# Second layer of an attention and expert kernel: an earlier token load, other places for the sinkhorn steps and weight splits, and three blocks rescaled on POOL

## The chip, the cores and the metric

The kernel runs on one core of a Trainium2 chip. The core has TensorE (PE: matrix products; its weight loads are shown apart as PEld), VectorE (DVE), ScalarE (ACT), GpSimd (POOL) and SyncE (SP), which here only issues DMAs. The metric is the device time of one execution in microseconds. The kernel before was run three times; of one more execution there is a profile.

## The reference

Three layers follow each other on 3072 tokens of width 512: chunked attention, an expert layer in which each token goes to at most one of 8 experts, and a second expert layer in which every token goes through all 8 experts, weighted by a matrix P that sinkhorn steps have balanced. The change lies in the last one:

```python
logits = x @ w_gate
P = np.exp(logits - logits.max())
for _ in range(8):
    P /= P.sum(1, keepdims=True) + 1e-09
    P /= P.sum(0, keepdims=True) + 1e-09
    P *= N / E
out = np.zeros((N, D))
for e in range(E):                       # 8 experts, D = 512, F = 1024
    ye = np.maximum(x @ w1[e], 0.0) @ w2[e]
    out += P[:, e:e + 1] * ye
```

All of it is in fp32. The kernel gets fp32 precision out of TensorE by splitting each operand into a high and a low part and adding three products.

## The kernel before

The order of the instructions of every engine is written out by hand; each engine runs its own in that order and waits on semaphores. A tile whose buffer is used again waits for the last user of that buffer.

**Blocks and units.** The second layer goes expert by expert (e) over six blocks of 512 tokens (s). Expert and block together are a block number b = 6e + s, and each has two halves of F, so unit n = 2b + half runs from 0 to 95; 12 units are an expert (`EU`). A product of 512x512 by 512x512 is made with seven products of quarter size instead of eight (Strassen's way): `h_mm(n, i)` is one of the seven products x @ w1 of unit n, `y_mm(n, i)` one of the seven h @ w2. Each is 12 matmuls of 128x256. In step n of the main loop (lines 1253 to 1315) TensorE makes the h products of unit n and, between them, the y products of unit n - 1, in the order `TURN` (line 40): h0, y, h1, y, h5, h4, y, h6, y, h3, h2, y, y, end. The y products come in the order `YORD`; the one behind h6 accumulates in the PSUM bank `y3`. In a step with even n two more y products follow (`y_tail`).

**What the other engines do in a step.** `h_done` (line 961) takes the h products out of PSUM: after h0 ACT copies the bank to a second one (line 964, called the seed copy here, since the further products are added onto it), after h6 VectorE adds r22 (line 954) and ACT and VectorE split it into high and low part (`c_hi`, `c_lo`: cb3), and after h2 VectorE makes the sum u (line 987) and four combinations that are split in turn. The bank of h0 is needed again by the next step's h0, so that waits for u; the bank of h3 waits for r22. In even steps `y_done` copies the first y product into the tile oB (ACT), and `y_end`, behind h0 of the next step, scales the parts of a block by P, adds them into oA and oB and stores them (`keep_out`): from block 6 on with an accumulating DMA issued by POOL (line 1058), before that with a DMA of SP.

**Blocks 0 and 1** of expert 0 are finished before P is known. They are kept unscaled in DRAM (`yd`), loaded later into oA and oB (`fix_load`), multiplied by P on VectorE and stored (`fix_store`), in steps 11 and 13.

**P.** `sink_max1` and `sink_exp` in step 1 take the maximum and the exponential, `sink_a` divides by the row sums. Each `sink_c` has a product with ones on TensorE into bank `y3` (line 901), then four VectorE operations; `sink_a` has four more. The eight steps lie in steps 3 and 5, behind h0, h1, h5 and h4 (lines 1230 to 1232).

**Later tokens.** During expert 0, odd steps prepare the next block: 16 transposes (`prep_trans`), four sums on POOL (`prep_sums`, into oA and oB), and seven splits (`prep_split`: ACT copies, VectorE subtracts), numbers 4 and 6 behind h2 and number 2 at the end. From block 5 on, `x_read` loads the seven split operands of the next block from DRAM in odd steps.

**Weights.** The eight pieces of the next expert are converted while the last unit of an expert and the first two of the next run: four subtractions on POOL for a piece (line 218), then four splits, each an ACT cast (line 204) and a VectorE subtraction (line 208). `QUOTA` (line 1251) says how many splits stand behind which h product, for n mod 12 = 11, 0 and 1.

**The start.** Lines 1149 to 1153 load the four w2 pieces of expert 0 into tiles that are needed later for other things; then line 1160 loads the first block's tokens (`x2n`, out of `x_t`, which the layer before fills by scatter DMAs of POOL), and line 1161 the logits (out of `l_t`, filled by further scatters). In unit 0 the h products go in the order `START` (0, 3, 1, 5, 6, 4, 2); lines 1203 to 1214 put sums and eight weight splits between them.

Of the kernel before, what the change touches and what calls it, by code (L numbers as in the profile page):

```python
# [8 lines left out]
F32 = mybir.dt.float32  # L9
# [4 lines left out]
ALU = mybir.AluOpType  # L14
# [20 lines left out]
EU = NS * 2  # L35
# [11 lines left out]
def kernel(ctx, tc, qT, kT, v, mem_kT, mem_v, wg, m1_w1, m1_w2, m2_w1, m2_w2, out):  # L47
    nc = tc.nc
# [291 lines left out]
    i = 0  # L340
# [505 lines left out]
    ones_f = m2.tile([128, 128], F32, name="ones_f")  # L846
    nc.gpsimd.memset(ones_f, 1.0)
    xd = [dram.tile([7, 128, 1024], F32, name=f"xd{s}") for s in range(NS)]
    yd = [dram.tile([2, 128, 1024], F32, name=f"yd{s}") for s in range(2)]
    add = lambda o, a, b: nc.vector.tensor_tensor(out=o, in0=a, in1=b, op=ALU.add)  # L850
    xn = {}
    xs = {}
# [1 line left out]
    def x2_load(sb):  # L854
        for h in range(2):
            xn[sb, h] = raw.tile([128, 2, D], F32, name="x2n", tag="wraw", bufs=3)
            r = 512 * sb + 256 * h
            nc.sync.dma_start(out=xn[sb, h], in_=x_t[r:r + 256, :].rearrange("(j p) d -> p j d", p=128))
# [41 lines left out]
    def sink_c(p):  # L900
        nc.tensor.matmul(p[:, 0:NT * E], ones_f, P.rearrange("p t e -> p (t e)"), start=True, stop=True)
        nc.vector.tensor_reduce(out=c_s, in_=p[:, 0:NT * E].rearrange("p (t e) -> p e t", e=E), axis=AX.X, op=ALU.add)
        nc.vector.tensor_scalar(out=c_s, in0=c_s, scalar1=1e-9, scalar2=float(E) / N, op0=ALU.add, op1=ALU.mult)
        nc.vector.reciprocal(out=c_s, in_=c_s)
        nc.vector.tensor_tensor(out=P, in0=P, in1=c_s.unsqueeze(1).to_broadcast(LS), op=ALU.mult)
# [28 lines left out]
    def h_mm(n, i, late=False):  # L934
        e, s, half = where_is(n)
        x = xs[s, i].rearrange("p h (k t) -> p h k t", k=2)
        new = i in (0, 4)
        if new:
            hb["a"] = bank("h_ps", "h0")
        p = hb["a" if i in (0, 1, 4, 2) else "b"]  # L940
        if late and i == 3:
            p, new = hb["d"], True
        if late and i == 0:
            nc.tensor.matmul(hb["b"], wt[E + e, 0, 0][0][:, 0, 0], xs[s, 0][:, 0], start=True, stop=True, skip_group_check=True)
        for f in range(2):
            wh, wl = wt[E + e, 0, 2 * half + f]
            o = p[:, 256 * f:256 * f + 256]
            for k in range(2):
                nc.tensor.matmul(o, wh[:, i, k], x[:, 0, k], start=(new and f == 0 and k == 0), stop=False, skip_group_check=True)  # L949
                nc.tensor.matmul(o, wh[:, i, k], x[:, 1, k], start=False, stop=False, skip_group_check=True)  # L950
                nc.tensor.matmul(o, wl[:, i, k], x[:, 0, k], start=False, stop=(k == 1), skip_group_check=True)  # L951
# [75 lines left out]
    def scaled(b, h, d, src):  # L1027
        e, s = divmod(b, NS)
        o = O[b, h][:, :, d]
        if b < 2:  # L1030
            if src is not None:
                nc.scalar.copy(out=o, in_=src)
            return
        for j in range(2):
            nc.scalar.activation(out=o[:, j], in_=(o if src is None else src)[:, j], func=ACTF.Copy, scale=P[:, 4 * s + 2 * h + j, e:e + 1])

    def plus(b, h, d, src):
        e, s = divmod(b, NS)
        o = O[b, h][:, :, d]
        if b < 2:  # L1040
            add(o, src, o)
            return
        for j in range(2):
            stt(o[:, j], src[:, j], P[:, 4 * s + 2 * h + j, e:e + 1], o[:, j], ALU.mult, ALU.add)
# [5 lines left out]
    def keep_out(b, h):  # L1050
        e, s = divmod(b, NS)
        o = O[b, h].rearrange("p j d f -> p j (d f)")
        if b < 2:
            nc.sync.dma_start(out=yd[s][h].rearrange("p (j d) -> p j d", j=2), in_=o)
        elif b < NS:
            nc.sync.dma_start(out=rows_of(s, h), in_=o)
        else:
            nc.gpsimd.dma_start(out=rows_of(s, h), in_=o, accum_op=ALU.add)  # L1058
# [35 lines left out]
    def fix_store(s):  # L1094
        for h in range(2):
            t = fixes[s, h].rearrange("p j d f -> p j (d f)")
            for j in range(2):
                nc.vector.tensor_scalar(out=t[:, j], in0=t[:, j], scalar1=P[:, 4 * s + 2 * h + j, 0:1], scalar2=None, op0=ALU.mult)
            nc.sync.dma_start(out=rows_of(s, h), in_=t)


# [45 lines left out]


    HOME = {0: ("cb5", 1, ("cb4",)), 1: ("cb2", 1, ("cb6",)), 2: ("cb1", 3, ("oA",)), 3: ("cb1", 3, ("wraw",))}
    for g in range(NG):  # L1150
        tag, bufs, _ = HOME[g]
        fetched[E, 1, g] = m2.tile([128, 1024], F32, name=tag, tag=tag, bufs=bufs)
        nc.sync.dma_start(out=fetched[E, 1, g], in_=m2_w2[0, g])
# [3 lines left out]
        d = [(raw if t == "wraw" else m2).tile([128, 1024], F32, name=t, tag=t, bufs=3 if t == "wraw" else 1) for t in tags]  # L1157
        conv_subs(E, 1, g, fetched[E, 1, g], (d[0][:, 0:512], d[0][:, 512:1024]))

    x2_load(0)  # L1160
    nc.sync.dma_start(out=P, in_=l_t.rearrange("(t p) e -> p t e", p=128))
    ps0 = {}
    for h, k in ((0, 0), (1, 0), (1, 1), (0, 1)):
# [29 lines left out]
    def start4():  # L1193
        x_hi(0, 2, sums[:, 0])

    def start2():
        x_lo(0, 2, sums[:, 0])

    between = {1: start5, 3: start6, 4: start4, 5: start2}
    hb["b"] = bank("h_ps", "h1")  # L1200
    hb["d"] = bank("h_ps", "y5")
    todo = []
    for k, i in enumerate(START):
        if k in between:
            between[k]()
        h_mm(0, i, True)
        h_done(0, i, True)
        if k in (3, 4):
            first_subs(k - 3)
            todo.append(w2_parts(E, k - 3))  # L1210
        if k in (4, 5):
            for q in todo:
                q.pop(0)()
                q.pop(0)()
# [12 lines left out]

    todo += [first_w2(2), first_w2(3)]
    sinks = {(1, "h0"): lambda p: (nc.vector.tensor_reduce(out=m_p, in_=P, axis=AX.XY, op=ALU.max), sink_max1(p)), (1, "h1"): sink_exp}
    for n in (3, 5):  # L1230
        for c in ("h0", "h1", "h5", "h4"):
            sinks[n, c] = sink_c if (n, c) == (5, "h4") else lambda p: (sink_c(p), sink_a())


    jobs = []
# [12 lines left out]
            todo.clear()  # L1248
            fetch()

    QUOTA = {EU - 1: {"h0": 2, "h1": 2, "h4": 2, "h6": 2}, 0: {"h0": 4, "h1": 4, "h4": 3, "h6": 3}, 1: {"h1": 3, "h4": 4, "h6": 3}}
    later = []
    for n in range(1, NU2 + 1):
        e, s, half = where_is(n)
        b = n // 2
        last = n == NU2
        m = n - 1
        k = n % EU
        nx = b + 1
        ends = half == 0  # L1260
        more = QUOTA.get(n if n < 1 else k, {})
        if n == EU - 2:
            limit[0] = len(order)
            for _ in range(3):
                fetch()
        if k == EU - 1 and e < E - 1:
            jobs += PIECES(e + 1)
            conv_subs(*jobs[0], fetched[jobs[0]])
        if n == 1:
            more = {"h0": 2, "h1": 2, "h5": 2, "h4": 2, "h6": 2}  # L1270
        assert n != 2 or not todo
        yq = list(YORD)
        if half == 0 and nx < NS and n > 1:
            x2_load(nx)
        prep = half == 1 and nx < NS
        for c in TURN:
            if c == "y":
                i = yq.pop(0)
                y_mm(m, i)
                if ends:  # L1280
                    y_done(m // 2, i)
            elif c == "end":
                if not last:
                    h_rest(n)
                    if prep:
                        prep_split(nx, 2)
                if ends and n > 1:
                    y_tail(m // 2)
                    later.append(lambda b=m // 2: y_end(b))
                if last:  # L1290
                    later.pop()()
                if n in (EU - 1, EU + 1):
                    fix_store((n - EU + 1) // 2)
            elif not last:
                i = int(c[1])
                h_mm(n, i)
                h_done(n, i)
                if later:
                    later.pop()()
                if (n, c) in sinks:  # L1300
                    sinks[n, c](bank("g_ps", "y3"))
                if n in (EU - 1, EU + 1) and c == "h4":
                    fix_load((n - EU + 1) // 2)
                if prep:
                    if c in ("h5", "h4"):
                        for h in range(2):
                            prep_trans(nx, h, ("h5", "h4").index(c))
                    if c == "h4":
                        prep_sums(nx)
                    for i in {"h6": (0, 1), "h3": (5, 3), "h2": (4, 6)}.get(c, ()):  # L1310
                        prep_split(nx, i)
                elif half == 1 and nx < E * NS:
                    x_read(nx % NS, i)
                for _ in range(more.get(c, 0)):
                    next_part()
# [43 lines left out]
```

## Time and profile before

| | |
|---|---|
| median of 3 runs | 2452.69 us (2451.85 to 2453.39) |
| the profiled execution | 2452.1 us, its span 2450.4 us |
| busy share of the span: PE, DVE, ACT, POOL | 95%, 62%, 49%, 21% |
| mean granted clock of TensorE | 0.978 of full speed |
| matmuls | 19522 |
| moved by DMA | 343 MB, 140 GB/s on the mean |

The span runs from the first to the last instruction of the profiled execution. The second layer fills it from about 380 us on. A row of the timeline gives the start, the duration, the engine, the line of the kernel, the operation, output<-input, the count of instructions that were merged, and in brackets the idle time of that engine just before and what ended it. A row of lines gives busy time and mean nanoseconds of one, and behind the second bar the idle time before them. A row of windows gives the two ends, the length, the busy time (and count) of PE, PEld, DVE, ACT and POOL, the granted clock, the busy share of the DMA engines and GB/s. Granted clock 1.00 is 2.4 GHz and 0.50 is 1.2 GHz.

### The profile page before, as it was taken

How to read it: one execution, taken by the hardware profiler on the slowest of the kernel's cores; microseconds unless marked ns; L12 is line 12 of the kernel's file. 1: busy time of each engine (PE TensorE's matmuls, PEld its weight loads, DVE VectorE, ACT ScalarE, POOL GpSimd, SP SyncE). 2: the span in 40 equal slices, each digit the busy share in tenths (PEclk: the TensorE clock that was granted, in tenths of full speed). 3: DMA queues.
4: the chain of work that ended last, by engine and by line, in shares of the span. 5: the costliest groups of instructions: out<-in, count | busy, mean ns of one | idle time of the engine just before them, and what ended most of it. 6: DMA issues, size and time to landing. Idle time of an engine off the chain costs nothing. (4 is left out here: it accounts for less than half of the span.)

```text
span 2450.4 us, 48134 instructions
## 1 busy us (share of the span) xinstructions
PE 2316.6 (95%) x19522; PEld 2268.6 (93%) x19522; DVE 1508.6 (62%) x2519; ACT 1200.4 (49%) x2488; POOL 509.4 (21%) x563
## 2 busy tenths in 40 slices
PE   8989994899989998999999999999999999999997
PEld 7879983889989998999899999999999999999997
DVE  5756564776785558555855585558555865576554
ACT  6744543445554445444544454445444554455443
POOL 4432233110230005000500050004101410141000
PEclk9989997999999999999999999999999999999999
DMA  9956643233462526353544355344534462535252
GB/s 236 255 147 200 203 135 133 95 128 140 151 245 79 155 82 177 121 144 90 164 138 123 111 145 157 103 130 133 169 95 138 122 180 82 151 121 155 79 155 35
DMA packets 154349, 343.25 MB, mean 140 GB/s; under 512 B 44489, under 2 KB 56905, under 8 KB 154123
## 3 DMA queue, kind: packets, MB, share of 16 engines
q1 hardware_dynamic: 128202, 289.35, 34.6%
q0 software_dynamic: 25920, 50.77, 12.4%
q8 instruction: 155, 2.54, 0.4%
q14 instruction: 72, 0.58, 0.1%
HBM read 256.71 MB, written 85.10 MB: 139 GB/s over the span
## 5 line engine op out<-in xcount | busy, mean ns | idle before, releaser
L949 PE MATMUL h_ps<-xs,wh 128*128 128x256 f32 x2688 | 766.9, 285 | 65.1 <-DVE r L850 46.3
L950 PE MATMUL h_ps<-xs,wh 128*128 128x256 f32 x2688 | 766.5, 285 | 0.0
L951 PE MATMUL h_ps<-xs,wl 128*128 128x256 f32 x2688 | 763.6, 284 | 0.0
L1018 PE MATMUL y_ps<-wh,cb 128*128 128x256 f32 x2304 | 650.7, 282 | 0.0
L1019 PE MATMUL y_ps<-wl,cb 128*128 128x256 f32 x2304 | 649.5, 282 | 0.0
L1020 PE MATMUL y_ps<-wh,cb 128*128 128x256 f32 x2304 | 648.2, 281 | 0.0
L949 PEld LDWEIGHTS h_ps<-xs,wh 128*128 128x128 f32 x2688 | 514.2, 191 | 72.2 <-DVE r L850 43.0
L951 PEld LDWEIGHTS h_ps<-xs,wl 128*128 128x128 f32 x2688 | 513.6, 191 | 0.0
L950 PEld LDWEIGHTS h_ps<-xs,wh 128*128 128x128 f32 x2688 | 511.5, 190 | 0.0
L915 DVE TENSOR_TENSOR cb<-r,cb 128x512 fp32r<-128x512 f32 x384 | 270.3, 713 | 278.1 <-ACT cb L925 272.0
L1020 PEld LDWEIGHTS y_ps<-wh,cb 128*128 128x128 f32 x2304 | 437.8, 190 | 0.0
L1018 PEld LDWEIGHTS y_ps<-wh,cb 128*128 128x128 f32 x2304 | 437.5, 190 | 0.0
L1019 PEld LDWEIGHTS y_ps<-wl,cb 128*128 128x128 f32 x2304 | 435.8, 189 | 0.0
L1058 POOL DMA_DIRECT2D out_dram<-oA x42 | 50.8, 1209 | 1362.6 <-ACT r L916 960.3
L925 ACT CAST cb<-r 128x512 fp32r<-128x512 f32 x384 | 239.4, 623 | 110.5 <-DVE r L917 86.5
L916 ACT ACTIVATE cb<-r 128x512 fp32r<-128x512 f32 x96 | 60.7, 632 | 288.0 <-DVE r L850 288.0
L916 ACT ACTIVATE r<-h_ps 128x512 f32<-128x512 f32 x191 | 114.3, 598 | 136.0 <-PE h_ps L951 135.3
L850 DVE TENSOR_TENSOR r<-h_ps,m 128x512 f32<-128x512 f32 x97 | 66.8, 689 | 180.5 <-PE h_ps L951 179.2
L208 DVE TENSOR_TENSOR wl<-wraw,wh 128x512 fp32r<-128x512 f32 (+2 forms) x150 | 144.4, 979 | 48.1 <-ACT wh L204 47.2
L218 POOL TENSOR_TENSOR wtt<-wraw 128x256 f32<-128x256 f32 x120 | 136.4, 1137 | 109.4 <-DVE wl L208 92.9
L964 ACT COPY h_ps<-h_ps 128x512 f32<-128x512 f32 x96 | 54.8, 571 | 197.9 <-PE h_ps L951 197.9
L915 DVE TENSOR_TENSOR r<-r,r 128x512 f32<-128x512 f32 x192 | 138.5, 722 | 3.3
(236 smaller groups left out, 3675.5 us busy)
## 6 DMA issues: line engine op xcount, KB each, us to landing
xs<-xd SPq DMA_DIRECT2D x294, 512.0 KB
wraw<-in_m_w_dram SPq DMA_DIRECT2D x124, 512.0 KB
xd<-xs SPq DMA_DIRECT2D x42, 512.0 KB
out_dram<-oA POOLq DMA_DIRECT2D x42, 512.0 KB, 6.3
out_dram<-oB POOLq DMA_DIRECT2D x42, 512.0 KB, 11.8
vw<-in_v_dram SPq DMA_DIRECT2D x40, 176.0 KB
qbd<-in_qT_dram SPq DMA_DIRECT2D x48, 128.0 KB
x_t<-x_nat SPq DMA_DIRECT2D x24, 256.0 KB
```

Source lines behind the costliest of these rows:

```text
L208: eng.tensor_tensor(out=lo, in0=src, in1=hi.bitcast(F32), op=ALU.subtract)
L218: sub = lambda o, a, b: nc.gpsimd.tensor_tensor(out=o, in0=a, in1=b, op=ALU.subtract)
L850: add = lambda o, a, b: nc.vector.tensor_tensor(out=o, in0=a, in1=b, op=ALU.add)
L915: tt = lambda o, a, b, op: nc.vector.tensor_tensor(out=o, in0=a, in1=b, op=op)
L916: relu = lambda o, i: nc.scalar.activation(out=o, in_=i, func=ACTF.Relu)
L925: (relu if pos else lambda o, i: nc.scalar.copy(out=o, in_=i))(cb[n, i][:, 0], src)
L949: nc.tensor.matmul(o, wh[:, i, k], x[:, 0, k], start=(new and f == 0 and k == 0), stop=False, skip_group_check=True)
L950: nc.tensor.matmul(o, wh[:, i, k], x[:, 1, k], start=False, stop=False, skip_group_check=True)
L951: nc.tensor.matmul(o, wl[:, i, k], x[:, 0, k], start=False, stop=(k == 1), skip_group_check=True)
L1018: nc.tensor.matmul(o, t[:, 0, c], wh, start=(i != 1 and half == f == j == 0), stop=False, skip_group_check=True)
L1019: nc.tensor.matmul(o, t[:, 0, c], wl, start=False, stop=False, skip_group_check=True)
L1020: nc.tensor.matmul(o, t[:, 1, c], wh, start=False, stop=(half == f == 1), skip_group_check=True)
```

## The change

Tokens first: `x2_load(0)` moves ahead of the four w2 loads on SP's queue. In unit 0 the eight weight splits move one product back (behind the product at place 5, and between the product at place 6 and its evacuation), and one subtraction (`x_lo(0, 2)`) moves ahead of the product at place 4. The eight sinkhorn steps lie behind h4 of step 1, h1, h4 and h6 of steps 3 and 5, and h1 of step 7. Block 2 is kept unscaled too; the three blocks are loaded, multiplied by P and stored in steps 11, 15 and 17, and the multiplication is on POOL. `prep_split` of numbers 4, 6 and 2 is put behind the seed copy of the next step. `QUOTA` moves splits from h1 and h4 to h6 and h3; their sum in each step stays.

```diff
-    yd = [dram.tile([2, 128, 1024], F32, name=f"yd{s}") for s in range(2)]
+    yd = [dram.tile([2, 128, 1024], F32, name=f"yd{s}") for s in range(3)]
...
     def scaled(b, h, d, src):
-        if b < 2:
+        if b < 3:
     def plus(b, h, d, src):
-        if b < 2:
+        if b < 3:
     def keep_out(b, h):
-        if b < 2:
+        if b < 3:
...
     def fix_store(s):
-                nc.vector.tensor_scalar(out=t[:, j], in0=t[:, j], scalar1=P[:, 4 * s + 2 * h + j, 0:1], scalar2=None, op0=ALU.mult)
+                nc.gpsimd.tensor_scalar(out=t[:, j], in0=t[:, j], scalar1=P[:, 4 * s + 2 * h + j, 0:1], scalar2=None, op0=ALU.mult)
...
+    x2_load(0)
     for g in range(NG):
         tag, bufs, _ = HOME[g]
...
-    x2_load(0)
     nc.sync.dma_start(out=P, in_=l_t.rearrange("(t p) e -> p t e", p=128))
...
     def start4():
         x_hi(0, 2, sums[:, 0])
-    def start2():
         x_lo(0, 2, sums[:, 0])
-    between = {1: start5, 3: start6, 4: start4, 5: start2}
+    between = {1: start5, 3: start6, 4: start4}
...
         h_mm(0, i, True)
+        if k == 6:
+            for q in todo:
+                q.pop(0)()
+                q.pop(0)()
         h_done(0, i, True)
         if k in (3, 4):
             first_subs(k - 3)
             todo.append(w2_parts(E, k - 3))
-        if k in (4, 5):
+        if k == 5:
             for q in todo:
                 q.pop(0)()
                 q.pop(0)()
...
-    for n in (3, 5):
-        for c in ("h0", "h1", "h5", "h4"):
-            sinks[n, c] = sink_c if (n, c) == (5, "h4") else lambda p: (sink_c(p), sink_a())
+    steps = [(1, "h4")] + [(n, c) for n in (3, 5) for c in ("h1", "h4", "h6")] + [(7, "h1")]
+    for c in steps:
+        sinks[c] = sink_c if c == steps[-1] else lambda p: (sink_c(p), sink_a())
...
-    QUOTA = {EU - 1: {"h0": 2, "h1": 2, "h4": 2, "h6": 2}, 0: {"h0": 4, "h1": 4, "h4": 3, "h6": 3}, 1: {"h1": 3, "h4": 4, "h6": 3}}
+    QUOTA = {EU - 1: {"h0": 2, "h1": 2, "h6": 3, "h3": 1}, 0: {"h0": 4, "h1": 3, "h4": 1, "h6": 4, "h3": 2}, 1: {"h1": 2, "h4": 2, "h6": 4, "h3": 2}}
+    FIX = {EU - 1: 0, EU + 3: 1, EU + 5: 2}
...
                     if prep:
-                        prep_split(nx, 2)
+                        later.append(lambda nx=nx: [prep_split(nx, i) for i in (4, 6, 2)])
...
-                if n in (EU - 1, EU + 1):
-                    fix_store((n - EU + 1) // 2)
+                if n in FIX:
+                    fix_store(FIX[n])
...
-                if n in (EU - 1, EU + 1) and c == "h4":
-                    fix_load((n - EU + 1) // 2)
+                if n in FIX and c == "h4":
+                    fix_load(FIX[n])
...
-                    for i in {"h6": (0, 1), "h3": (5, 3), "h2": (4, 6)}.get(c, ()):
+                    for i in {"h6": (0, 1), "h3": (5, 3)}.get(c, ()):
```

## Rows read from the trace of the kernel before

**Rows 1.** The page: busy time, share of the span, instructions.
```profile
PE 2316.6 (95%) x19522; PEld 2268.6 (93%) x19522; DVE 1508.6 (62%) x2519; ACT 1200.4 (49%) x2488; POOL 509.4 (21%) x563
```

**Rows 2.** Windows, seed copy to seed copy: length, busy by engine, clock, DMA.
```profile
471.60:501.44 29.84, 25.36 (x192) 24.37 (x190) 24.00 (x53) 12.18 (x23) 5.54 (x4) 0.94 0.27 106
...
573.28:596.26 22.98, 22.11 (x184) 21.52 (x182) 15.08 (x24) 13.82 (x28) 5.53 (x4) 1.00 0.36 138
...
680.00:708.69 28.69, 24.30 (x182) 24.09 (x181) 22.70 (x35) 14.77 (x31) 11.42 (x12) 0.88 0.41 142
728.36:756.68 28.32, 24.25 (x183) 24.05 (x182) 12.99 (x22) 8.28 (x15) 0.00 (x0) 0.88 0.23 90
756.68:775.28 18.60, 18.60 (x159) 18.60 (x158) 10.17 (x18) 9.42 (x18) 2.60 (x2) 1.00 0.86 233
...
916.90:937.47 20.57, 19.13 (x161) 18.93 (x160) 18.01 (x24) 13.00 (x26) 14.40 (x14) 1.00 0.92 270
937.47:963.94 26.47, 22.90 (x180) 22.70 (x180) 22.20 (x34) 14.83 (x30) 13.78 (x12) 0.94 0.22 69
963.94:984.16 20.22, 18.87 (x159) 18.67 (x158) 17.31 (x29) 13.82 (x29) 6.32 (x6) 1.00 0.91 263
984.16:1005.61 21.45, 21.45 (x183) 21.45 (x182) 11.36 (x18) 8.61 (x15) 0.00 (x0) 1.00 0.12 49
```

**Rows 3.** Timeline of all engines, 370 to 430 us.
```profile
370.06 0.98 POOL L764 DMA_INDIRECT x_t<-x2e,rid  x1 [2.50 <-DVE x2e L763]
...
379.12 0.99 POOL L794 DMA_INDIRECT l_t<-l,rid  x1 [1.39 <-DMA l_t<-l,rid]
...
381.74 1.75 SPq L1153 DMA_DIRECT2D cb<-in_m_w_dram  x4
383.60 1.19 SPq L858 DMA_DIRECT2D x2n<-x_t  x2
...
391.19 1.11 PE L880 MATMUL x_ps<-ident,x2n 128*128 128x128 f32 x4 [18.43 <-DMA x2n<-x_t]
```

**Rows 4.** Timeline of SP and ACT, units 13 and 14.
```profile
731.64 0.39 SPq L1099 DMA_DIRECT2D out_dram<-oB  x1
...
736.68 0.84 ACT L1035 ACTIVATE oB<-y_ps,P 128x256 f32<-128x256 f32 x2 [7.75 <-DMA out_dram<-oB]
```

**Rows 5.** Timeline of VectorE and TensorE, unit 0.
```profile
406.72 4.39 DVE L208 TENSOR_TENSOR wl<-cb,wh 128x512 fp32r<-128x512 f32 x4 [1.20 <-ACT wh L204]
...
412.99 0.55 PE L949 MATMUL h_ps<-xs,wh 128*128 128x256 f32 x1 [7.39 <-DVE r L850]
...
417.71 0.68 DVE L850 TENSOR_TENSOR u<-h_ps,u 128x512 f32<-128x512 f32 x1
```

**Rows 6.** Waits of TensorE, 376 to 680 us: total, times, longest.
```profile
PE g_ps L901 <- DVE P L898: 7.8, 4, 2.0
PE h_ps L949 <- ACT h_ps L964: 5.8, 5, 1.2
```

**Rows 7.** Timeline of VectorE: first and last of one step's eight operations.
```profile
474.05 0.35 DVE L902 TENSOR_REDUCE r_s<-g_ps 128x8 f32<-128x192 f32 x1
...
476.21 0.36 DVE L898 TENSOR_TENSOR P<-P,r_s 128x192 f32<-128x192 f32 x1
```

**Rows 8.** Groups by line and shape, VectorE: the low part of cb3.
```profile
L917 DVE SCALAR_TENSOR_TENSOR cb<-r,cb 128x512 fp32r<-128x512 f32 x96 | 71.6, 745 | 67.0 <-ACT cb L916 67.0
```

**Rows 9.** Timeline of POOL, ACT and TensorE in unit 24.
```profile
942.63 3.27 POOL L218 TENSOR_TENSOR wtt<-wraw 128x256 f32<-128x256 f32 x1 [5.18 <-DVE wl L208]
...
948.12 0.62 ACT L204 CAST wh<-wtt 128x512 fp32r<-128x512 f32 x1 [3.12 <-POOL wtt L218]
...
952.11 0.58 PE L949 MATMUL h_ps<-xs,wh 128*128 128x256 f32 x1 [3.57 <-DVE r L850]
```

**Rows 10.** Groups by line and shape, POOL: the slowest of the sums for later tokens.
```profile
L1135 POOL TENSOR_TENSOR oB<-x2T,oA 128x512 f32<-128x512 f32 x5 | 8.2, 1646 | 0.0
```

**Rows 11.** DMA issues, 755 to 790 us: count, KB each, us to landing.
```profile
out_dram<-oB POOLq DMA_DIRECT2D x1, 512.0 KB, 12.4
```

## The prediction

> **What bounds the kernel now.** I read the page's busy line first: TensorE is busy for 95% of the span [rows 1], so a gain can only come out of the 5% in which it stands still. Then the windows of single units of the second layer, cut at the seed copies. A unit that nothing disturbs takes 18.60 us (odd) or 21.45 us (even), with TensorE busy throughout [rows 2]. Three kinds of unit are longer: those of the sinkhorn steps (29.84), those that prepare later tokens (22.98), and those at the change of an expert (20.57, 26.47, 20.22, and at the first change 28.69 and 28.32) [rows 2]. In these the VectorE column is what to look at. Before unit 0 TensorE stands still for 18.43 us [rows 3]. So the bound is TensorE, with VectorE (and POOL and the queue of SP behind it) setting the end in those stretches. The forecast is made against the profiled execution, 2452.1 us (span 2450.4, 1.7 around it); the median of the runs is 2452.69, 0.6 above.
>
> **Token loads first.** The four w2 loads are issued at 381.74, the moment after the last scatter of l_t (POOL, 379.12) has landed, and the loads of x2n stand behind them on SP [rows 3]. x2n reads x_t alone, whose last scatter went out at 370.06; POOL's second l_t scatter began 2.4 us after the start of the first (0.98 of issue, then 1.39 of wait) [rows 3], so x_t is landed at 372.5, or 374 if a scatter of whole rows takes longer. SP is free then. Two stores of 512 KB landed 5.0 us after the second's issue (731.64 to 736.68) [rows 4]; taken for the two loads, the transposes begin at about 378 (377 to 379.5) and not at 391.19: 13 us earlier (11.7 to 14.2). Where it is moved past: the w2 loads lose nothing, since they can't leave before 381.7; their users on POOL move forward by the same 13 us, to about 387, 5 us after the issue, so cover remains, and up to 1 us could be lost there. I take 13.
>
> **First weights after the fourth product.** TensorE waits 7.39 us before the last product of unit 0, for a sum that VectorE makes only after four weight splits of 4.39 us together, which began at 406.72 [rows 5]. Moved behind, the product starts at once, but the next unit needs the sum u, which VectorE made at 417.71 after all of these operations [rows 5]. The chain is VectorE's, and its operations stay the same; the new order fills the 1.20 us that VectorE waits in front of the splits, and about half a microsecond more among them. I take 1.8 (0 to 3). The move of one subtraction ahead of a product is in this. Sum of the start: 14.8 us.
>
> **Sinkhorn steps.** The waits for P cost 7.8 us in four waits [rows 6]; the chain of eight VectorE operations of one step takes 2.5 us (474.05 to 476.57) [rows 7]. An undisturbed odd unit has 13 products in 18.60 us, 1.43 each; steps at h0, h1, h5 and h4 are one or two of them apart. After the change none are less than two apart (2.9 us), and these waits go. Two things come in their place. A step at h6 writes bank y3, and the next y product needs that bank: it waits until VectorE has read it, behind r22 (0.68, as u [rows 5]), VectorE's wait for ACT's part of cb3 (67.0 us over 96 such waits, 0.70 each) and its own part (0.75) [rows 8], and a reduction (0.35 [rows 7]): 2.5 us, in units 3 and 5. And VectorE's work remains: walking its operations in order, the copy that opens the next unit's y comes 3.6 us earlier than now, in each of the two units (bounds 1 and 6.9; the upper is the excess of 29.84 over 22.98 [rows 2]). Against it stands one step in unit 1, where VectorE is the chain: 2.5 us, and 0.35 in unit 7. Sum 7.2 - 2.9 = 4.3 us (-2 to 9).
>
> **Later tokens' sums behind the seed copy.** TensorE waited for the seed copy 5.8 us in 5 waits [rows 6]. The copy now goes first; but ACT's first copy out of y into oB must wait for the same three subtractions, as they read oB, and these are at the end of VectorE's chain as before. So most of it comes back one product later: I take 0.25 us a unit, 1.2 in all (0 to 5.8).
>
> **Quotas at the change of an expert.** Three units of 67.26 us stand where 18.60 + 21.45 + 18.60 = 58.65 would do: 8.6 us, six times (the last one 6.9): 49.4 us. The waits: TensorE stands 3.57 us for r22, behind three weight splits, behind ACT, which waits 3.12 for POOL's subtractions, whose first takes 3.27 [rows 9]. The change leaves one split ahead of r22 in that unit, none in the unit before it, and puts six (four in the unit before) behind it, where the next thing TensorE needs is the sum u. VectorE is busy for 18.01 + 22.20 + 17.31 = 57.5 us of the three units [rows 2]; with the 0.70 wait for ACT in each [rows 8] that is 59.6, so not over 7.6 of the 8.6 can be won unless work spills into the fourth unit. Walked by hand with 0.69 us a split: the first unit keeps its 2 us, because u is as late as now; the second loses 0.2; the third loses 0.9, where six splits stand between r22 and u. Left over 3.1, won 5.5 a change, 4 in the last: 31.5 us (lower bound nothing, upper 7.6 a change: 44). The first change is counted with the next part.
>
> **Three blocks rescaled later, on POOL.** What is removed: the stalls of units 12 and 14, which lie 7.24 and 6.87 us above 21.45 [rows 2]. In unit 14 ACT waited 7.75 us for the store of oB [rows 4], TensorE stood still behind it, and after that it ran for a while at the lower level of 1.2 GHz (granted clock 0.88 over the unit [rows 2]). What is added: the same stores in units 11, 15 and 17. In unit 11 the 512 KB transfers ahead of it on the queue end the store, not the multiply, so I leave 5 of the 7.24 there (1 to 7). POOL's multiply has no row: the slowest group of two-operand POOL operations on 128x512 takes 1.65 us [rows 10], VectorE 0.68 for such a one [rows 5]. I take 1.2, nearer the first, since the engine is the same; in unit 11 it lies beside the queue's transfers, and in units 15 and 17 two of the four lie behind the accumulate's landing. In units 15 and 17 the block before is stored with an accumulating DMA, which landed 12.4 us after its issue [rows 11]; fix_load needs the same tile, so SP waits for it to about 17 us into an 18.60 us unit, with the four last x_read loads queued behind SP. DMA is already busy 0.86 of that unit [rows 2]. Load of oB, four x_reads, two stores: seven transfers of about 1.3 us (5.0 for two, less 2.4 until the first byte) end 9 to 12 us into the next unit, and ACT's first y copy waits for that. In unit 14 ACT was released 8.3 us in (736.68 against 728.36) and the unit lost 6.87. So 8 us each (5 to 10.5; nothing if the accumulate lands some 6 us sooner once the x_reads are out of its way). Sum: 5 + 16 - 14.1 = 7 us lost (-14 to +12). That one block more is kept unscaled costs nothing: one ACT copy for two, and VectorE's plain sums are of the same length.
>
> **How it comes together.** 2452.1 - 14.8 - 4.3 - 1.2 - 31.5 + 7 = 2407.3; I say 2407.
>
> **A rule weighed.** POOL's first subtraction took 3.27 us while VectorE ran splits back to back [rows 9]. The Trainium skill, "SBUF — State Buffer", section "Who interferes with whom", says that a VectorE instruction with two SBUF inputs and a GpSimd instruction that reads SBUF exclude each other for a whole instruction. By that rule the four subtractions for the piece due at h3, which now run beside the moved splits, would each wait out one split, and what it would do here is rival 4.
>
> **The rivals.**
> 1. VectorE's work is conserved: the moved splits delay u by as much as they freed r22, and no transition shrinks. For it: 57.5 us of VectorE in units that should take 58.65. Against it: VectorE and ACT sat idle over 3 us for POOL in the second unit [rows 9]. Price: the 31.5 don't come: 2439.
> 2. Less is left over than I count: the accumulates land early, so the fixes hide (21 us less), or the transitions clear fully (18 less). For it: an even unit has the DMA busy for 0.12 of it [rows 2]. About 2387.
> 3. The load does not do what it says: x2n is still held, by a buffer or by l_t. Against it: w2's wait is for memory that the scatters' indices lay in, x2n's is another pool. 13 us less won: 2420.
> 4. POOL starves beside the moved splits. Four subtractions each waiting 0.69 are 2.7 us late, 1.4 more than the slack of u in the walk: 10 us over seven changes, 2417. If ACT and VectorE then stand in line for them as in the 3.12 us wait, in two units of a change, unit 14's loss of 6.87 us, low clock included, comes twice: 13.7 in place of 3.1 a change, 74 us: 2481, **slower**. It decides from a loss of 10.5 us a change (8.6, and the 13 us won elsewhere over seven). Against it: in the walk the pieces' buffers come free some 4 us before the pieces are due.
>
> **How the numbers follow.** Forecast 0.46 (its own range 2395 to 2420), rival 1 0.2, rival 2 0.2, rival 3 0.06, rival 4 0.08 (half of it the slower end). The range that leaves out 2 in 10 goes from 2380, the lower half of rival 2, to 2440, past rival 1. Within 0.2% (about what a measurement of this kernel can tell from no change; 2448 to 2457) lies the tail of rival 1 with a start that moves less: 0.03. Slower: 0.04. Faster: 0.93.
>
> **What would show it.** Right: the first transposes near 378; in the windows of the three transition units together 62 us and not 67, VectorE's busy time unchanged; a new wait of a y product for a reduction, twice 2.5; units 14 back to 21.45 and units 16 and 18 at 27 to 30 with ACT waiting for a store of oB. Wrong: transition units still at 67 (rival 1), 16 and 18 at 21.45 (rival 2), SP's first load of x2n at 381 (rival 3), or a longer ACT wait for POOL ahead of u (rival 4).

## The result, and the profile after

The changed kernel takes 2413.68 us (median of four runs, 2411.26 to 2418.49), the kernel before 2452.27 beside it; the ratio is 0.9846 (95% interval 0.9827 to 0.9864). The profiled execution of the changed kernel took 2411.26 us, 40.8 less than that of before. 2407 was forecast, with a range of 2380 to 2440.

The page of the changed kernel: span; busy time, share and instructions; two groups of matmuls with the idle time before them.

```profile
span 2409.5 us, 48142 instructions
...
PE 2314.5 (96%) x19522; PEld 2264.0 (94%) x19522; DVE 1512.9 (63%) x2508; ACT 1198.0 (50%) x2482; POOL 530.5 (22%) x575
...
L949 PE MATMUL h_ps<-xs,wh 128*128 128x256 f32 x2688 | 766.7, 285 | 43.5 <-ACT r L916 18.7
...
L1018 PE MATMUL y_ps<-wh,cb 128*128 128x256 f32 x2304 | 652.2, 283 | 6.9 <-DVE r_s L902 4.6
```

TensorE's busy time is 2.1 us below that of before [rows 1], the span 40.9 us: 38.8 us of standing still are gone. Where, the windows of single units tell, seed copy to seed copy: units 3, 12, 14, 16 and the change of an expert 23 to 26 (columns as in [rows 2]).

```profile
457.58:483.17 25.59, 23.27 (x181) 22.74 (x180) 20.36 (x44) 10.63 (x19) 5.47 (x4) 0.93 0.33 124
...
658.01:688.18 30.17, 23.40 (x183) 23.19 (x182) 19.10 (x29) 14.81 (x29) 20.75 (x20) 0.89 0.40 140
707.21:728.24 21.03, 21.03 (x179) 21.03 (x178) 12.13 (x19) 8.62 (x16) 0.00 (x0) 1.00 0.14 56
...
746.85:776.50 29.65, 23.74 (x183) 23.54 (x182) 11.99 (x19) 8.28 (x15) 5.66 (x4) 0.88 0.27 101
...
904.18:924.95 20.77, 20.19 (x168) 19.78 (x166) 18.21 (x24) 13.05 (x27) 14.57 (x14) 1.00 0.91 270
924.95:946.92 21.97, 21.34 (x179) 21.34 (x180) 20.53 (x29) 14.74 (x30) 13.74 (x12) 1.00 0.25 82
946.92:966.91 19.99, 19.22 (x157) 18.60 (x156) 19.02 (x33) 13.84 (x29) 6.12 (x6) 1.00 0.81 229
966.91:987.91 21.00, 20.92 (x176) 20.72 (x175) 12.14 (x19) 8.63 (x16) 0.00 (x0) 1.00 0.21 83
```

Set beside [rows 2]: unit 3 fell from 29.84 to 25.59, unit 14 from 28.32 to 21.03, the change of an expert (23 to 26) from 88.71 to 83.73. Unit 12 did not fall (28.69, now 30.17), and unit 16, 21.45 before, lost 8.2 us; unit 18 lost 7.5 in the same way.

Layers ahead of the second one shift from execution to execution: the last scatter of x_t starts at 369.32 here, at 370.06 before [rows 3], and at up to 373.5 in the runs below. So all comparisons below are of distances between seed copies (the starts of line 964 in ACT's timeline), and the start is measured from that scatter. The forecast's terms and what the two traces show:

| term, us | forecast | trace after against before |
|---|---|---|
| start: load first | -13 | -15.0 (scatter to seed copy 0: 27.4, now 12.4) |
| start: order in unit 0 | -1.8 | 0.0 (unit 0: 23.53, now 23.57) |
| sinkhorn and later sums, units 1 to 10 | -5.5 | -6.1 (240.27, now 234.13) |
| three blocks and first change, units 11 to 18 | +7 | +9.1 (175.53, now 184.65) |
| quotas, from unit 19 on | -31.5 | -28.1 (1571.42, now 1543.32) |
| layers ahead | 0 | -0.7 |
| sum | -44.8 | -40.8 |

### The profile page after: what moved, and what is told of

It is laid out like the page before. It is cut to its first block, busy times and chain, and to the rows that moved or that the text cites. A ratio compares the mean times of both kernels' runs of the same rounds, so it can differ in the third digit from the quotient of the medians.

```text
span 2409.5 us, 48142 instructions
## 1 busy us (share of the span) xinstructions
PE 2314.5 (96%) x19522; PEld 2264.0 (94%) x19522; DVE 1512.9 (63%) x2508; ACT 1198.0 (50%) x2482; POOL 530.5 (22%) x575
## 4 chain that ended last, share of the span: by engine, by line
PE 70%; DVE 10%; issue 8%; DMA 6%; ACT 3%; POOL 2%; SPq 0%; POOLq 0%; ACTq 0%; DVEq 0%
PE h_ps L949 11%; PE h_ps L950 11%; PE h_ps L951 10%; PE y_ps L1018 10%; PE y_ps L1019 10%; PE y_ps L1020 10%; DVE wl L208 4%; DMA qbd<-in_qT_dram 2%; DMA out_dram<-oB 2%; DVE r L915 1%; PE s_ps L271 1%; PE h_ps L739 1%; PE h_ps L740 1%; PE h_ps L738 1%; PE y_ps L756 1%
## 5 line engine op out<-in xcount | busy, mean ns | idle before, releaser
L218 POOL TENSOR_TENSOR wtt<-wraw 128x256 f32<-128x256 f32 x120 | 130.2, 1085 | 92.2 <-DVE wl L208 82.8
```

Of the source, the lines that this page charges most:

```text
L218: sub = lambda o, a, b: nc.gpsimd.tensor_tensor(out=o, in0=a, in1=b, op=ALU.subtract)
```

## Experiments: one part undone at a time

Each of these is one execution with a profile; they are read by units, not by their total time. Some units differ between runs that have the same code in them: unit 0 takes 23.5 to 23.9 us, units 3 and 5 take 24.2 or 25.4 to 25.6, unit 12 takes 28.65 to 30.17, unit 16 29.35 to 30.93 and unit 18 28.77 to 29.67. A difference inside such a spread says nothing about the edit.

**The load.** The token loads stand behind the w2 loads again.

```diff
-    x2_load(0)
     for g in range(NG):
...
+    x2_load(0)
     nc.sync.dma_start(out=P, in_=l_t.rearrange("(t p) e -> p t e", p=128))
```

> The changed kernel with one part undone: the first block's token loads stand behind the four w2 loads on SP again. Theory (the place on the queue is worth the whole of the start): SP issues x2n at about 383 us again, the first transposes move from 375.3 to about 391, the seed copy of unit 0 from 381.7 to about 397, and everything behind it moves by the same 15 us; time about 2427 (2425 to 2430). Rival (x2n would be held by something else soon after, so that the early issue alone wins only a part, and the rest came from the new order in unit 0): the seed copy of unit 0 moves by less than 12 us and unit 0 itself changes by 2 us or more.

2424.98 us. Scatter to seed copy 0 is 27.0 us, 14.6 more than in the changed kernel; unit 0 stays at 23.5. The changed kernel's SP and TensorE first, then the same instructions here:

```profile
371.54 0.91 SPq L858 DMA_DIRECT2D x2n<-x_t  x2
380.94 1.77 SPq L1154 DMA_DIRECT2D cb<-in_m_w_dram  x4
...
375.27 1.12 PE L880 MATMUL x_ps<-ident,x2n 128*128 128x128 f32 x4 [3.25 <-DMA x2n<-x_t]
```

```profile
383.63 1.75 SPq L1153 DMA_DIRECT2D cb<-in_m_w_dram  x4
385.50 1.19 SPq L858 DMA_DIRECT2D x2n<-x_t  x2
...
393.09 1.11 PE L880 MATMUL x_ps<-ident,x2n 128*128 128x128 f32 x4 [18.46 <-DMA x2n<-x_t]
```

The place on the queue is the whole of it: TensorE's 18.46 us shrink to 3.25. In the changed kernel the tokens were there 3.7 us after SP's issue, not 5. The total is 2 us short of the theory's 2427: units 1 to 18 came out 4.7 us shorter than in the changed kernel, most of it in units 3, 5 and 12 (1.2 to 1.4 each, as they do between runs; for units 3 and 5 see the last section), and the layers ahead 2.6 longer.

**The order in unit 0.** The eight splits and `x_lo(0, 2)` go back to where they stood.

```diff
-        if k == 6:
...
         h_done(0, i, True)
...
-        if k == 5:
+        if k in (4, 5):
```

> The changed kernel with one part undone: in unit 0 the eight weight splits stand where they stood, behind the products at places 4 and 5, and the subtraction x_lo(0, 2) is behind the former again. By the prediction's walk unit 0 (seed copy 0 to seed copy 1) gets 1.8 us longer, 25.4 and not 23.6. Theory now: the new order is worth nothing, because VectorE has the same operations in front of the sum u and the moved splits run beside POOL's subtractions: 23.6, within 0.5. Time within 2 us of the changed kernel either way.

2414.88 us; unit 0 takes 23.72, inside the 23.5 to 23.9 that it takes with the new order: the order is worth nothing that these runs can show. The waits of TensorE (total, times, longest) between 370 and 440 us with the old order, then between 400 and 440 us with the new one:

```profile
PE h_ps L949 <- DVE r L850: 10.8, 2, 7.4
...
PE h_ps L949 <- DVE u L850: 2.5, 1, 2.5
```

```profile
PE h_ps L949 <- DVE u L850: 9.9, 1, 9.9
PE h_ps L949 <- DVE r L850: 3.4, 1, 3.4
```

7.4 + 2.5 has become 9.9: the wait moved behind the product and kept its length. The prediction wanted 1.8 us of VectorE's gaps back. VectorE did close them, but its splits got longer. In the changed kernel, and then the last three splits with the old order:

```profile
393.60 4.61 DVE L208 TENSOR_TENSOR wl<-cb,wh 128x512 fp32r<-128x512 f32 x4
398.12 0.94 DVE L208 TENSOR_TENSOR vl<-cb,vh 128x256 fp32r<-128x256 f32 x1
398.99 1.21 DVE L208 TENSOR_TENSOR wl<-cb,wh 128x512 fp32r<-128x512 f32 x1
400.12 0.94 DVE L208 TENSOR_TENSOR vl<-cb,vh 128x256 fp32r<-128x256 f32 x1
```

```profile
404.23 0.68 DVE L208 TENSOR_TENSOR wl<-cb,wh 128x512 fp32r<-128x512 f32 x1
404.83 0.41 DVE L208 TENSOR_TENSOR vl<-cb,vh 128x256 fp32r<-128x256 f32 x1
405.17 0.68 DVE L208 TENSOR_TENSOR wl<-cb,wh 128x512 fp32r<-128x512 f32 x1
```

In the changed kernel POOL was making subtractions until 400.8, and each split of 128x512 beside them took 1.1 to 1.2 us; the one after that took 0.68. With the old order POOL was done at 404.0, before these three. VectorE's busy time in unit 0 is 18.07 us with the old order and 19.83 with the new.

**The quotas.** The old QUOTA.

```diff
-    QUOTA = {EU - 1: {"h0": 2, "h1": 2, "h6": 3, "h3": 1}, 0: {"h0": 4, "h1": 3, "h4": 1, "h6": 4, "h3": 2}, 1: {"h1": 2, "h4": 2, "h6": 4, "h3": 2}}
+    QUOTA = {EU - 1: {"h0": 2, "h1": 2, "h4": 2, "h6": 2}, 0: {"h0": 4, "h1": 4, "h4": 3, "h6": 3}, 1: {"h1": 3, "h4": 4, "h6": 3}}
```

> The changed kernel with one part undone: the old QUOTA. Theory (the quotas alone shorten the changes of an expert, by 5.0 us in the three units of a change and 3.4 in the last): from seed copy 20 to seed copy 95 it takes 28 us more; time about 2440. Rival (VectorE's work is conserved, and what shortened the changes was something else in the change): seed copies 20 to 95 as far apart as in the changed kernel, within 3 us. The first change (units 11 to 13), where the rescaling lies too: between 0 and 5 us more.

2443.53 us; from unit 19 on it takes 1571.45 us, 28.1 more, and units 11 to 18 take 2.8 more (1.3 of it in units 13 and 14, most of the rest in unit 16, which no quota touches). From unit 19 on the quotas alone are the gain, and the idea that VectorE's work is conserved (rival 1) falls. TensorE's waits from 842 us on in the changed kernel, and from 868 us on with the old quotas:

```profile
PE h_ps L949 <- ACT h_ps L964: 8.3, 12, 1.1
PE y_ps L1018 <- ACT oA L1035: 2.3, 6, 0.4
```

```profile
PE h_ps L949 <- DVE r L850: 37.7, 18, 3.6
```

The 18 waits for r22 are gone (37.7 us), and 10.6 us of others have come, most of them for the seed copy.

**The multiply.** On VectorE again, same places and buffers.

```diff
-                nc.gpsimd.tensor_scalar(out=t[:, j], in0=t[:, j], scalar1=P[:, 4 * s + 2 * h + j, 0:1], scalar2=None, op0=ALU.mult)
+                nc.vector.tensor_scalar(out=t[:, j], in0=t[:, j], scalar1=P[:, 4 * s + 2 * h + j, 0:1], scalar2=None, op0=ALU.mult)
```

> The changed kernel with the three blocks multiplied by P on VectorE and not on POOL; places and buffers as in the changed kernel. Theory (POOL's multiplies, 1.5 to 2.4 us each, four in a row, stand on the path from the load to the store): unit 12 gets 2 to 5 us shorter (30.2 to 25 to 28), units 16 and 18 get 3 to 4 us shorter each (29.6 and 29.0 to about 26 and 25.5); sum 8 to 13 us, time about 2401. Rival (the prediction's: in units 15 to 18 the landing of the accumulate and the seven transfers behind it set the end): units 16 and 18 within 1 us of 29.6 and 29.0, and only unit 12 moves.

2414.76 us. Unit 12 takes 28.75 and unit 16 30.69, both inside the spread of the runs that multiply on POOL; only unit 18, with 26.60, is shorter than in any of them, by 2.2 to 3.1. Over units 11 to 18 it is 2.2 us less than in the changed kernel, where the theory wanted 8 to 13. It fell: the stalls stay without POOL's multiply, which is a part of the one in unit 18. Unit 16 shows why. In the changed kernel (SP, POOL, SP, ACT, TensorE; seed copy at 746.85):

```profile
743.53 0.32 SPq L1092 DMA_DIRECT2D oB<-yd  x1
743.94 1.82 SPq L875 DMA_DIRECT2D xs<-xd  x4
...
744.91 4.52 POOL L1098 TENSOR_SCALAR oA<-oA,P 128x512 f32<-128x512 f32 x2 [9.41 <-issue]
749.41 3.10 POOL L1098 TENSOR_SCALAR oB<-oB,P 128x512 f32<-128x512 f32 x2
...
752.54 0.39 SPq L1099 DMA_DIRECT2D out_dram<-oB  x1
...
757.01 0.84 ACT L1035 ACTIVATE oB<-y_ps,P 128x256 f32<-128x256 f32 x2 [9.59 <-DMA out_dram<-oB]
...
758.39 0.58 PE L949 MATMUL h_ps<-xs,wh 128*128 128x256 f32 x1 [5.91 <-ACT r L916]
```

With the multiply on VectorE (seed copy at 750.14):

```profile
753.36 0.39 SPq L1099 DMA_DIRECT2D out_dram<-oB  x1
...
761.20 0.84 ACT L1035 ACTIVATE oB<-y_ps,P 128x256 f32<-128x256 f32 x2 [10.49 <-DMA out_dram<-oB]
```

The store of oB is issued 3.2 us after the seed copy instead of 5.7, and yet lands no sooner: 11.1 after it instead of 10.2 (9.6 to 10.9 in the other runs). When it is issued, the four token loads and the first store stand ahead of it, and the DMA engines stay 0.99 busy for another 4.2 us. In unit 18 the store's issue moved from 6.3 to 3.0 us after the seed copy and its landing from 9.3 to 7.6. Which of the two ends last differs from unit to unit, as the prediction's seven transfers had it for unit 16.

**The sinkhorn steps.** Back to the dense places of before.

```diff
-    steps = [(1, "h4")] + [(n, c) for n in (3, 5) for c in ("h1", "h4", "h6")] + [(7, "h1")]
+    steps = [(n, c) for n in (3, 5) for c in ("h0", "h1", "h5", "h4")]
```

> The changed kernel with one part undone: the eight sinkhorn steps stand behind h0, h1, h5 and h4 of units 3 and 5 again. Prediction: units 3 and 5 get 3.6 us longer each, unit 1 2.5 us shorter, unit 7 0.35 shorter; 4.3 us more in all. Theory now, from the trace of the changed kernel: units 3 and 5 back to 29.8 (4.2 longer each), unit 1 1.2 shorter, unit 7 as it is; 7 us more from seed copy 1 to seed copy 11. Rival (the units' lengths follow the later tokens' sums and not the steps): less than 2 us.

2417.74 us. Units 3 and 5 get 2.4 and 3.6 us longer (27.97 and 29.23), unit 1 2.3 shorter, unit 7 0.35 shorter: 3.4 from seed copy 1 to 11. This is one execution, and the clock can move units 3 and 5 by 1.4 each (last section). The prediction's 4.3 is nearer than the 7 that I read out of the changed trace afterwards; that reading had put down to the steps a part of what the later tokens' sums had won.

**The later tokens' sums.** Splits 4, 6 and 2 ahead of the seed copy again.

```diff
-                        later.append(lambda nx=nx: [prep_split(nx, i) for i in (4, 6, 2)])
+                        prep_split(nx, 2)
...
-                    for i in {"h6": (0, 1), "h3": (5, 3)}.get(c, ()):
+                    for i in {"h6": (0, 1), "h3": (5, 3), "h2": (4, 6)}.get(c, ()):
```

> The changed kernel with one part undone: the splits 4, 6 and 2 for later tokens stand behind h2 and at the end of the unit again, ahead of the seed copy. Prediction: 1.2 us more over five units (0 to 5.8), unit by unit 0.25. Theory now: in the changed kernel the waits of TensorE for the seed copy in units 1 to 9 are gone, but units 8 and 10 are 0.7 longer and units 7 and 9 0.7 to 1.1 shorter than before, so odd units get longer by 0.7 to 1.1 and even ones shorter by 0.4 to 0.7; within 2 us in all.

2414.34 us. Odd units 3 to 9 get 1.1 longer each and unit 1 0.7, even ones 0.45 to 0.75 shorter: 2.1 more in all, where 1.2 was forecast. That most of it comes back in the next unit was right.

## Experiments: what the changed kernel still loses

**Tiles of their own.** The three blocks no longer pass through oA and oB.

```diff
-            fixes[s, h] = o_tile(h)
+            fixes[s, h] = raw.tile([128, 2, 512], F32, name="x2T", tag="wtt", bufs=2)
...
-    FIX = {EU - 1: 0, EU + 3: 1, EU + 5: 2}
+    FIX = {EU + 2: 0, EU + 4: 1, EU + 6: 2}
...
-                if n in FIX:
-                    fix_store(FIX[n])
...
-                if n in FIX and c == "h4":
+                if n in FIX and c == "h0":
                     fix_load(FIX[n])
+                if n in FIX and c == "h4":
+                    fix_store(FIX[n])
```

> The changed kernel, but the three blocks are loaded into two tiles of their own (the tag wtt, which the weights leave free from unit 14 on) and not into oA and oB, at h0 of units 14, 16 and 18, multiplied on POOL and stored behind h4 of the same unit. Theory (the 8 us that units 16 and 18 lose, and the part of unit 12 above a normal change of an expert, are nothing but ACT's wait for the store of oB): units 14, 16 and 18 take 21.45 each, unit 12 comes down from 30.2 to between 22 and 25; 20 to 24 us in all, time about 2391 (ratio to the kernel before 0.974 to 0.976). Rival (the transfers and POOL's multiplies disturb the units wherever they stand, by the accumulate next to them or by VectorE's operations beside POOL's): units 14, 16 and 18 longer than 23 us each, less than 15 us won.

2388.23 us (median of four runs, 2386.88 to 2390.34); ratio to before 0.9733 (0.9713 to 0.9752). Units 12, 14, 16 and POOL's four multiplies in unit 16:

```profile
657.13:679.12 21.99, 21.99 (x186) 21.93 (x185) 20.57 (x29) 14.74 (x31) 13.74 (x12) 1.00 0.25 82
698.68:719.68 21.00, 20.94 (x176) 20.74 (x176) 12.14 (x19) 8.61 (x17) 7.02 (x4) 1.00 0.41 159
738.28:759.74 21.46, 21.46 (x183) 21.46 (x182) 11.16 (x18) 8.60 (x16) 6.19 (x4) 1.00 0.30 119
...
741.33 6.19 POOL L1098 TENSOR_SCALAR x2T<-x2T,P 128x512 f32<-128x512 f32 x4 [14.40 <-DMA x2T<-yd]
```

The same loads, multiplies and stores cost units 12, 14, 16 and 18 nothing here. Units 12, 16 and 18 gave back 23.9 us, the wait for the store of oB and the low clock behind it (granted 0.88 and 0.89 in the changed kernel, 1.00 here); units 11 and 13 took 0.5 more each, so 22.8 in all. The edit moves two things at once, the tile and the place (from odd units, beside the accumulates and the token loads, into even ones). In the new places it is the tile that counts: in unit 16 the stores are issued from 6.2 us after the seed copy on, later than in the changed kernel, and ACT writes oB 1.4 us after it, without a wait for them. What tiles of their own would be worth in the old places no run shows.

**Two steps a unit.** Only unit 5's step behind h6 moves, to unit 7.

```diff
-    steps = [(1, "h4")] + [(n, c) for n in (3, 5) for c in ("h1", "h4", "h6")] + [(7, "h1")]
+    steps = [(1, "h4"), (3, "h1"), (3, "h4"), (3, "h6")] + [(n, c) for n in (5, 7) for c in ("h1", "h4")]
```

> The changed kernel with the sinkhorn steps in other places: one behind h4 of unit 1, three in unit 3 as before (h1, h4, h6), two each in units 5 and 7 (h1, h4). Only unit 5 loses its step behind h6, and with it the wait of a y product for the bank y3. Theory (that wait of 2.3 us and the low clock behind it, 1.4 us, are what three steps cost over two; VectorE has room for two): unit 5 comes from 25.6 to about 22, unit 7 stays within 0.7 of 22.2; 2.5 to 4 us won. Rival (VectorE's work is what counts, wherever the steps are): unit 7 gets longer by as much as unit 5 gets shorter, within 1 us.

2412.43 us. Units 5 and 7:

```profile
508.17:530.40 22.23, 22.16 (x185) 21.74 (x184) 18.53 (x36) 10.72 (x20) 5.54 (x4) 1.00 0.35 135
551.90:574.10 22.20, 22.14 (x185) 21.72 (x184) 16.58 (x32) 10.73 (x20) 5.53 (x4) 1.00 0.35 136
```

Unit 5 came from 25.59 to 22.23, unit 7 stayed at 22.2. A second step costs such a unit nothing (unit 7 has one step in the changed kernel and takes 22.24). The third costs 3.4 us, 2.0 where the clock stays up (24.2 in the run with the load put back). Whether it is the number of steps or the place behind h6, where the next y product needs bank y3, no run separates.

**Both, and a fourth block.** On the kernel with tiles of their own:

```diff
-        if b < 3:
+        if b < 4:
...
-    steps = [(1, "h4")] + [(n, c) for n in (3, 5) for c in ("h1", "h4", "h6")] + [(7, "h1")]
+    steps = [(n, c) for n in (3, 5, 7, 9) for c in ("h1", "h4")]
...
-    FIX = {EU + 2: 0, EU + 4: 1, EU + 6: 2}
+    FIX = {EU + 2: 0, EU + 4: 1, EU + 6: 2, EU + 8: 3}
```

> The kernel with tiles of their own for the rescaled blocks, with two edits more: block 3 is kept unscaled too (rescaled in unit 20), so that P may be ready as late as unit 9, and the eight sinkhorn steps stand two a unit, behind h1 and h4 of units 3, 5, 7 and 9. Theory (an odd unit of this stretch hides two steps and not three, a step in unit 1 costs its own VectorE time, and a rescaled block costs nothing in an even unit with its own tiles): unit 1 2.3 us shorter, units 3 and 5 at 22.2 each (3.3 shorter), unit 7 as it is, unit 9 within 0.5 of 21.9, unit 20 at 21.45; about 8.7 us less than 2388.2: 2379.5 (ratio to the kernel before 0.970). Rival (VectorE's eight steps cost the same wherever they stand): what units 1, 3 and 5 win comes back in units 7 and 9, and the time stays within 3 us of 2388.

2382.38 us (median of five runs, 2379.41 to 2384.78); ratio to before 0.9711 (0.9698 to 0.9724). Units 3, 9 and 20:

```profile
454.93:477.17 22.24, 22.17 (x185) 21.75 (x184) 18.54 (x36) 10.74 (x20) 5.54 (x4) 1.00 0.35 136
...
586.12:608.35 22.23, 22.15 (x185) 21.73 (x184) 16.60 (x32) 10.72 (x19) 5.54 (x4) 1.00 0.35 136
...
810.50:831.94 21.44, 21.44 (x183) 21.44 (x182) 11.22 (x18) 8.61 (x15) 6.20 (x4) 1.00 0.25 97
```

From seed copy 1 to 11 it takes 225.03 us, 8.7 less than with three blocks, as the theory had it. Units 7 and 9 are 22.23 each, so what units 1, 3 and 5 won comes back there only as 0.3 in unit 9. The medians of the two are 5.9 apart and the profiled executions 8.2; the intervals of their ratios overlap, so between these two it is the units that decide. Against the kernels before and after the change this one is the fastest.

## Why the prediction was right, step by step

**Load: right, 2 us short.** Transposes at 375.27, not 378; behind the last scatter of x_t that is 6.0 us and not 7.9. The term mis-sized is in the main the landing: 5.0 us were taken from two stores [rows 4]; these two loads took 3.7. The other 0.7 is SP's issue, 2.2 us after that scatter where about 2.9 was taken.

**Order in unit 0: wrong by its whole size, 1.8 us.** The step that failed is "its operations stay the same". They are the same in number, but beside POOL's subtractions they are longer. With the old order the last three come when POOL is done: 0.68, 0.41 and 0.68, against 1.21, 0.94 and 0.68.

**Sinkhorn: right (4.3 forecast, 3.4 by undoing it).** The new wait was named with its place and its size: a y product behind a reduction, twice 2.5; it is 2.3 twice, and it ends with the reduction of line 902 behind r22 and cb3, in that order. What the sum did not have is the clock: behind that wait it is low for a while, 1.4 us in each of the two units (last section); unit 3 of before was granted 0.94 too [rows 2]. The old places of the steps cost unit 3 less than I thought (2.4, not 3.6).

**Sums behind the seed copy: right in kind, 0.9 short.**

**Quotas: right, 3.4 us too much.** In the change 23 to 26 the walk left over 3.1 us (2, 0.2 and 0.9); measured are 2.2, 0.5 and 1.4, less 0.45 in the fourth unit. So 5.0 are won a change and not 5.5, 3.4 in the last and not 4. That the last one had only 6.9 to lose before was the clock and not the change of an expert (last section). VectorE's 57.5 us in the first three units [rows 2] stayed 57.8.

**Three blocks: right in units 14, 16 and 18, wrong in unit 12.** Units 16 and 18 lost 8.2 and 7.5 where 8 each was forecast, out of the chain that was forecast: accumulate, load, token loads, store, ACT. In unit 12 I left 5 us of the stall, since "the 512 KB transfers ahead of it on the queue end the store, not the multiply"; it is 8.7 above 21.45. The multiply, taken as 1.2 us with bounds of 0.68 and 1.65, is 2.2 on the mean there:

```profile
656.85 4.85 POOL L1098 TENSOR_SCALAR oA<-oA,P 128x512 f32<-128x512 f32 x2 [6.96 <-DMA oA<-yd]
661.68 4.11 POOL L1098 TENSOR_SCALAR oB<-oB,P 128x512 f32<-128x512 f32 x2
...
665.82 0.39 SPq L1099 DMA_DIRECT2D out_dram<-oB  x1
...
669.03 0.84 ACT L1035 ACTIVATE oB<-y_ps,P 128x256 f32<-128x256 f32 x2 [8.56 <-POOL wtt L218]
...
670.41 0.58 PE L949 MATMUL h_ps<-xs,wh 128*128 128x256 f32 x1 [6.77 <-ACT r L916]
```

The store goes out 7.8 us after the seed copy (658.01), and ACT gets oB 11.0 after it. (The row puts ACT's wait down to a subtraction of POOL on another tile; that it is for the store is read from the run with tiles of their own, where ACT got oB 2.4 after the seed copy.) With VectorE's multiply the store went out 4.6 us after the seed copy, ACT got oB 8.7 after it, and unit 12 was still 28.75, much the same as the 28.69 of before. So the step that failed is the 2.2 us taken off the stall: nothing in the change took them off. The other 1.5 of the 3.7 missed are in this trace POOL's, but with POOL's multiply the unit takes 28.65 to 30.17 from run to run, so that its price there lies between nothing and 1.5.

**Rivals.** 1 falls by the quotas' run. 2 falls: the accumulate of oB landed 9.7 us after its issue in unit 15, sooner than the 12.4 of [rows 11], but units 16 and 18 lost 8 all the same, and the changes of an expert kept 3.6 us. 3 falls by the load's run. Of 4 the mechanism exists, in unit 0 and in units 23 and 24, where splits beside POOL's subtractions take up to 1.3 us; but r22 and u had room for it, and the changes of an expert got shorter. The errors cancelled in part: 3.3 us too little for the load, units 1 to 10 and the layers ahead, 7.3 too much for quotas, order and blocks.

## What to carry over

A step that loads, changes and stores something through a tile that an evacuation needs next cost the whole round trip here, whichever engine did the arithmetic: look for a tile, and a place, that is idle in that stretch before moving the arithmetic to another engine. A dependent chain on VectorE stayed hidden here with two steps in a unit and not with three, so spread it by unit and not by product, and away from a bank that the next product needs. And when work is moved behind the wait that it caused, see which wait is next on the same engine: in unit 0 the same 9.9 us were there, one product later.

## What the runs showed of the chip

**A POOL multiply by a column of P** on 128x512 took 1.56 us where VectorE was nearly idle (the four in 6.19 us above), and 2.2 to 2.6 beside its splits and combinations in units 11, 12, 15 and 17. The extra 0.65 to 1.1 us is about one VectorE operation with two inputs or somewhat more (a split of 128x512 took 0.68 where POOL stood idle). This agrees with the Trainium skill, "SBUF — State Buffer", section "Who interferes with whom", by which a VectorE instruction with two SBUF inputs contends with a GpSimd instruction that reads SBUF, and the ports that they share are an exclusive lock. In unit 0 both pay: VectorE's splits took 1.2 us in place of 0.68, POOL's subtractions of 128x256 up to 1.2 in place of 0.73. It does not show each time: one VectorE operation of that kind fell into the four of 6.19 us, took 0.69, and none of the four got longer.

**The same wait cost 2.3 us or 3.7.** In unit 3 TensorE waited 2.31 us for bank y3 in the changed kernel, and 2.30 in the run with the load put back. Windows of 1.6 us behind that wait, the changed kernel first:

```profile
473.58:475.18 1.60, 1.60 (x10) 1.60 (x9) 1.43 (x6) 0.00 (x0) 0.00 (x0) 0.50 0.04 10
```

```profile
490.22:491.82 1.60, 1.60 (x16) 1.60 (x15) 1.43 (x6) 0.00 (x0) 0.00 (x0) 1.00 0.04 10
```

In the first TensorE ran at its lower level, 1.2 GHz (10 matmuls where the other made 16; the windows on either side were granted 0.77 and 0.67), and the unit had it busy 1.4 us longer; in the second it stayed at 2.4 GHz, and units 3 and 5 took 24.2 in place of 25.6. The instructions of the unit and the wait are the same; what decided it, the runs don't show. The change of an expert shows the same where the quotas are the old ones. TensorE waits 3.6 us for r22 in its second unit; that unit then took 26.4 to 26.5 us, granted 0.94, in five of the six changes (unit 24 in [rows 2] is one), and 24.9 to 25.0 in the sixth, granted 1.00. In the kernel before it was the last change, in the run with the old quotas the first of these six:

```profile
2181.56:2206.50 24.94, 21.38 (x180) 21.17 (x180) 20.70 (x31) 14.61 (x30) 13.78 (x12) 1.00 0.22 74
```

```profile
928.43:953.39 24.96, 21.33 (x180) 21.13 (x179) 20.70 (x31) 14.72 (x31) 13.82 (x12) 1.00 0.24 73
```

A stall of this length is therefore priced with both ends.
